# Retention and mixture of experts in one kernel: the loads of q, k and v from batch 1 on divided into 17 transfers a batch instead of 6

## The chip, the cores and the metric

The kernel runs on one core of one Trainium2 chip. The metric is the device time of one execution in microseconds (us); less is better. Engines are named as the profile names them: PE (matrix multiply) with PEld (its weight loads), DVE (VectorE), ACT (ScalarE), POOL (GpSimd) and SP (SyncE, which here only issues DMA transfers).

## The reference

A retention layer (8 batches, 8 heads, 576 positions, head size 64) feeds a mixture of experts with one expert per token (4608 tokens of 512 values, 8 experts, hidden size 1024). All data are float32.

```python
# retention, for each batch and head
scores = q @ k.T / sqrt(64)
gamma  = 1 - 2**(-5 - head)
D[i, j] = gamma**(i - j) if i >= j else 0
x = (scores * D) @ v                    # -> tokens of 8 * 64 = 512 values
# mixture of experts
xn, en = x / (|x| + 1e-6), emb / (|emb| + 1e-6)
logits = xn @ en.T / tau
e      = argmax(logits)                 # one expert a token
gate   = max(softmax(logits))
out    = gate * (relu(x @ w1[e]) @ w2[e])
```

## The kernel before, in words

The program has two stages. The retention stage is a loop over eight batches b. The expert stage follows it; it gathers the tokens of each expert and multiplies them with that expert's weights. Within each engine the order of the instructions is the order in which the Python code emits them (`manual_schedule`), SP's queue included; the semaphores between the engines are placed by the framework.

Work of one batch b in the retention stage, with the names that occur in the profile:

- `load_batch(b)` issues the batch's loads on SP: `load_qk` (L475) brings q and k, transposed, of one pair of heads p into a tile `qkt` (8 buffers, so two batches of four pairs); `load_v` (L488) brings v into `vt` (2 buffers), whose last 256 columns are the tail of positions 512 to 575; `load_k` (L483) brings k by chunks of 128 positions into `kt` (2 buffers). The order is pairs 0 and 1, v, k, pairs 2 and 3. `load_batch(1)` stands ahead of the loop, and `load_batch(b + 2)` at the end of batch b, since its buffers are those that batch b has just read.
- Batch 0 is different: its loads are cut finer and spread over SP and ACT, and its k by chunks is made on the chip (L608, L610), not loaded.
- `scale_k(b)` (L600) multiplies `kt` by a factor per position on POOL, one instruction for each of four chunks of 512 columns. It is emitted near the end of batch b - 1. `scale_q` (L619) does the same for the q of a pair, on POOL, too.
- `emit_A` (L630 on PE, L639 on DVE) makes the decayed scores of a pair; `emit_U` (L657) the products of k and v by chunk, four groups of 16 matmuls, of which each reads one chunk of the scaled `kt` and of `vt`; `emit_O` (L713) and `emit_S` (L729) the output of two pairs; `emit_At` and `emit_Ot` (L751, L768) that of the tail.
- The tokens of batch b are turned during batch b + 1 (`route_tile`, L794 on PE), copied by ACT into one of five buffers `y` in rotation (L798) and stored by SP to the scratch tensor `xd` in device memory (L800). SP also issues a quarter of an expert's first weights (L459) in batches 2 to 5.

SP works through its list in order: when a transfer has to wait (for its buffer, or for a semaphore), everything behind it waits as well. The transfers of SP's and ACT's queues use eight semaphores in rotation (DMAHW0 to DMAHW7 below), so a transfer is issued only when the one eight places earlier has landed.

```python
def load_batch(b):
    load_qk(b, 0); load_qk(b, 1)
    load_v(b); load_k(b)
    load_qk(b, 2); load_qk(b, 3)
```

Of the kernel before, what the change touches and what calls it, by code (L numbers as in the profile page):

```python
# [19 lines left out]
B, H, S, D = 8, 8, 576, 64  # L20
NP = H // 2
# [3 lines left out]
DM = H * D  # L25
# [59 lines left out]
def retention_moe(ctx: ExitStack, tc: tile.TileContext, qk, kv, w1, w2, head, cst, out):  # L85
    nc = tc.nc
# [12 lines left out]
    def cc(name):  # L99
        o, w = _C[name]  # L100
        return cs[:, o : o + w] if o < _FIRST else late["cd"][:, o - _FIRST : o - _FIRST + w]
# [346 lines left out]
    with ExitStack() as att:  # L448
# [20 lines left out]
        def load_qk(b, p):  # L469
            t = qkp.tile([P, 2, S], F32, name="qkt")  # L470
            if b == 0:
                for i, on in enumerate(both):
                    on.dma_start(out=t[:, i], in_=qk[b, p, :, i])
            else:
                nc.sync.dma_start(out=t, in_=qk[b, p])  # L475
            qkt[b, p] = t

        kt, vt_ = {}, {}
        KW = NCH * DM

        def load_k(b):
            t = a1.tile([P, KW], F32, name="kt", bufs=2)
            nc.sync.dma_start(out=t, in_=kv[b, :, :KW])  # L483
            kt[b] = t

        def load_v(b):
            t = a2.tile([P, KW + NP * D], F32, name="vt")
            nc.sync.dma_start(out=t, in_=kv[b, :, KW:])  # L488
            vt_[b] = t

        cd = late["cd"] = ap.tile([P, _CST.shape[1]], F32, name="cd")
# [12 lines left out]
        o = _C["g1"][0] - _FIRST  # L504
        nc.sync.dma_start(out=cs, in_=head)
        load_qk(0, 0)
        load_decay(0, 2 * P, nc.scalar)
        load_qk(0, 1)
        load_decay(o, _CST.shape[1] - o)
        load_decay(2 * P, 2 * P, nc.scalar)  # L510
        for i, on in enumerate(both):
            c = slice(2 * i, 2 * i + 2)
            on.dma_start(out=v0[:, c, : DM // 2], in_=v1[:, c, : DM // 2])
        load_qk(0, 2)
        load_decay(4 * P, 2 * P)
        load_decay(6 * P, 2 * P, nc.scalar)
# [361 lines left out]
        def load_batch(b):  # L878
            load_qk(b, 0)
            load_qk(b, 1)  # L880
            load_v(b)
            load_k(b)
            load_qk(b, 2)
            load_qk(b, 3)
# [57 lines left out]
        b = B - 1  # L942
# [19 lines left out]
    with ExitStack() as moe:  # L962
# [272 lines left out]
        b = B - 1  # L1235
# [53 lines left out]
    with tc.If(ntile > 0):  # L1289
        with ExitStack() as ov:  # L1290
# [9 lines left out]
                out=io8, in0=cc("iota")[:, :NE], scalar1=float(ES), scalar2=None, op0=ALU.mult  # L1300
# [4 lines left out]
                out=sel, in0=eidx_all.unsqueeze(2).broadcast_to([P, NT, NE]), in1=io8, op=ALU.is_equal  # L1305
            )
            nc.vector.tensor_tensor(
                out=sel, in0=sel, in1=ovs[:, :NE].unsqueeze(1).broadcast_to([P, NT, NE]), op=ALU.mult
# [12 lines left out]
                out=tok, in0=entry[:, :, 0], scalar1=float(P), scalar2=cc("part"), op0=ALU.mult, op1=ALU.add  # L1321
            )
            nc.vector.tensor_scalar(out=tok, in0=tok, scalar1=float(1 - P), scalar2=None, op0=ALU.add)
            for t in range(NT):
                nc.gpsimd.indirect_dma_start(
                    out=od[:, :],
                    out_offset=bass.IndirectOffsetOnAxis(ap=dsti[:, t : t + 1], axis=0),
                    in_=tok[:, t : t + 1],
# [8 lines left out]
                out=te,  # L1337
# [10 lines left out]
            with tc.For_i(0, ntile, 1) as i:  # L1348
# [9 lines left out]
                    out=of[:, 0:1], in0=ent[:, 0:1], scalar1=-1.0, scalar2=0.0, op0=ALU.add, op1=ALU.max  # L1358
                )
                nc.vector.tensor_scalar(  # L1360
                    out=of[:, 2:3], in0=ent[:, 0:1], scalar1=0.0, scalar2=BIG, op0=ALU.is_equal, op1=ALU.mult
# [6 lines left out]
                    out=go,  # L1368
                    out_offset=None,
                    in_=gd[:, :],  # L1370
# [4 lines left out]
                    out=xo,  # L1375
                    out_offset=None,
                    in_=xd[:, :],
# [8 lines left out]
                for f4 in range(NF // 4):  # L1386
                    ph = psm.tile([P, 512], F32, name="m")
                    for fi in range(4):
                        f = 4 * f4 + fi
                        for d in range(NP):  # L1390
                            o = BLK[f // NPR][d // 2] * 256 + d % 2 * P
# [11 lines left out]
                for f in range(NF):  # L1403
# [4 lines left out]
                    out=out[:, :],  # L1408
                    out_offset=bass.IndirectOffsetOnAxis(ap=oi[:, 1:2], axis=0),
                    in_=yo,  # L1410
# [61 lines left out]
```

## Time and profile before

| what | value |
|---|---|
| runs | 583.46, 584.24, 584.25 us (median 584.24) |
| profiled execution, time | 583.77 us |
| its span in the trace | 581.9 us (1.87 us lie around it) |
| retention stage | about 0 to 150 us of the span |
| PE busy | 568.6 us, 98% of the span |
| granted PE clock | full (0.999) |
| batch loads on SP from batch 1 on | 28 of `qkt` (576 KB), 7 of `vt` (1152 KB), 7 of `kt` (1024 KB) |

The share of PE is an average over two very different stages. In the retention stage both PE and the 16 DMA engines are nearly full; in the expert stage the DMA engines are busy a little over half of the time. In the tables of stretches the column "DMA share" is the mean busy share of the 16 DMA engines by their packets, and the last column what they moved. A row of the chain of waits names what the last instruction of the program waited for, step by step backwards.

### The profile page before, as it was taken

Reading aid. Unit: us, or ns where it says so; the run is one execution under the profiler, and the core shown is the slowest. Engines: PE = TensorE matmul, PEld = TensorE weight load, DVE = VectorE, ACT = ScalarE, POOL = GpSimd, SP = SyncE. Lnnn points to the kernel's source line nnn. Section 1 sums busy time; section 2 is a strip of 40 time slices with the busy share of each in tenths; the row PEclk is TensorE's granted clock in tenths of the full one; section 3 lists DMA queues with packets and bytes.
Section 4 is the critical chain, followed back from the end, with each engine's and each line's share of the span. In section 5 each row is a group of like instructions: output and inputs, shape, how many; then the busy total and the mean of one; then the engine's idle time right before and its main releaser. Section 6 shows DMA issues by size and latency. Waiting matters only on the chain.

```text
span 581.9 us, 13055 instructions
## 1 busy us (share of the span) xinstructions
PE 568.6 (98%) x5096; PEld 508.0 (87%) x5096; DVE 413.9 (71%) x829; ACT 383.6 (66%) x718; POOL 306.3 (53%) x303
## 2 busy tenths in 40 slices
PE   8999999999999999999999999999999999999995
PEld 7788888788899899889988988998899899889985
DVE  3566776667685768787877878787878778786800
ACT  1344656554748887788788778878877887876511
POOL 4474444654455668567457636645773665345021
PEclk9999999999999999999999999999999999999999
DMA  8999999972568367457544845655394366422211
GB/s 299 396 357 374 361 376 331 388 285 79 184 192 202 113 183 169 129 162 171 169 126 138 179 133 157 167 166 143 127 190 138 113 186 172 120 98 99 75 41 44
DMA packets 72689, 109.58 MB, mean 188 GB/s; under 512 B 42378, under 2 KB 44462, under 8 KB 70832
## 3 DMA queue, kind: packets, MB, share of 16 engines
q1 hardware_dynamic: 63248, 86.53, 47.7%
q0 software_dynamic: 7680, 19.95, 10.8%
q10 hardware_dynamic: 1696, 2.23, 1.2%
q8 instruction: 41, 0.67, 0.5%
q14 instruction: 24, 0.20, 0.1%
HBM read 80.62 MB, written 19.94 MB: 173 GB/s over the span
## 4 chain that ended last, share of the span: by engine, by line
PE 78%; issue 7%; DMA 5%; DVE 5%; ACT 3%; POOL 1%; SPq 0%; POOLq 0%; ACTq 0%; DVEq 0%
PE m L1154 33%; PE a L1103 14%; PE m L1103 10%; PE a L630 5%; PE m L713 4%; PE a L413 3%; PE m L794 3%; PE m L657 2%; DMA kt<-kv 2%; PE m L729 2%; PE m L821 1%; DMA cd<-cst 1%; ACT w2s L1003 1%; DMA qkt<-qk 1%; DVE hs L1069 1%
## 5 line engine op out<-in xcount | busy, mean ns | idle before, releaser
L1154 PE MATMUL m<-w2s,hs 128*128 128x512 f32 (+1 forms) x984 | 221.0, 385 | 0.4 <-DVE hs L1069 0.4
L1154 PEld LDWEIGHTS m<-w2s,hs 128*128 128x128 f32 x984 | 180.7, 188 | 38.3 <-DVE hs L1069 2.5
L1164 POOL DMA_INDIRECT out<-y,sid x40 | 43.0, 1075 | 88.7 <-ACT y L1163 63.2
L1028 POOL TENSOR_TENSOR wsum<-raw 128x256 f32<-128x256 f32 x56 | 44.1, 811 | 56.4 <-DVE hs L1069 22.3
L619 POOL TENSOR_TENSOR qkt<-qkt,gsb 128x448 f32<-128x448 f32 x32 | 36.9, 1170 | 55.1 <-PE a L630 45.4
L330 POOL DMA_INDIRECT gt<-gd,gid x40 | 50.9, 1274 | 17.1 <-issue 10.2
L1103 PE MATMUL a<-xsb,w0s 128*128 128x320 f32 x324 | 54.8, 309 | 0.0
L319 POOL DMA_INDIRECT raw<-xd,gid x40 | 39.4, 986 | 27.3 <-DVE xsb L403 16.8
L1115 DVE TENSOR_TENSOR y<-m,y 128x320 f32<-128x320 f32 x84 | 40.9, 487 | 17.4 <-PE m L1103 9.4
L1069 DVE SCALAR_TENSOR_TENSOR hs<-y,hs 128x320 fp32r<-128x320 f32 x84 | 47.5, 584 | 6.6 <-ACT hs L1074 5.5
L399 ACT CAST xsb<-raw 128x128 fp32r<-128x128 f32 x70 | 32.1, 459 | 30.2 <-DVE raw L382 29.2
L1074 ACT ACTIVATE hs<-y 128x320 fp32r<-128x320 f32 x84 | 38.9, 472 | 18.0 <-DVE y L1115 17.5
L1119 ACT COPY y<-a 128x320 f32<-128x320 f32 x84 | 35.7, 425 | 22.7 <-PE a L1103 12.4
L639 DVE TENSOR_TENSOR raw<-a,cd 128x512 f32<-128x512 f32 x64 | 39.9, 683 | 14.0 <-PE a L630 14.0
L1103 PEld LDWEIGHTS a<-xsb,w0s 128*128 128x128 f32 x324 | 49.4, 188 | 0.1
L1006 DVE TENSOR_TENSOR w2s<-raw,w2s 128x1024 fp32r<-128x1024 f32 x32 | 39.6, 1239 | 13.1 <-ACT w2s L1003 13.1
L364 ACT COPY raw<-raw 128x1024 uint16<-128x1024 uint16 x35 | 47.5, 1356 | 0.0
L375 DVE TENSOR_TENSOR raw<-raw 128x256 f32<-128x256 f32 x35 | 22.0, 628 | 35.5 <-ACT raw L364 35.5
L1163 ACT ACTIVATE y<-m,gt 128x512 f32<-128x512 f32 (+1 forms) x41 | 27.6, 673 | 23.7 <-PE m L1154 23.5
L403 DVE TENSOR_TENSOR xsb<-raw,xsb 128x128 fp32r<-128x128 f32 x70 | 39.3, 594 | 1.1 <-ACT xsb L399 0.6
L1003 ACT CAST w2s<-raw 128x1024 fp32r<-128x1024 f32 x32 | 33.5, 1046 | 7.8 <-DMA raw<-w 7.7
L630 PE MATMUL a<-qkt 64*128 64x128 f32 x512 | 34.7, 280 | 2.6 <-DMA qkt<-qk 1.5
(176 smaller groups left out, 1124.3 us busy)
## 6 DMA issues: line engine op xcount, KB each, us to landing
raw<-w SPq DMA_DIRECT2D x64, 512.0 KB, 3.7
qkt<-qk SPq DMA_DIRECT2D x28, 576.0 KB, 11.5
xd<-y SPq DMA_DIRECT2D x36, 256.0 KB, 11.2
vt<-kv SPq DMA_DIRECT2D x7, 1152.0 KB, 9.3
kt<-kv SPq DMA_DIRECT2D x7, 1024.0 KB, 10.7
qkt<-qk ACTq DMA_DIRECT2D x4, 288.0 KB, 4.4
qkt<-qk SPq DMA_DIRECT2D x4, 288.0 KB, 5.8
raw<-xd,gid POOLq DMA_INDIRECT x40, 4.0
```

What stands on the lines that cost most here:

```text
L319: nc.gpsimd.indirect_dma_start(out=t[:, XO : XO + DM], out_offset=None, in_=xd[:rows, :], in_offset=bass.IndirectOffsetOnAxis(ap=gid[:, a ...
L330: nc.gpsimd.indirect_dma_start(out=g[:, i : i + 1], out_offset=None, in_=gd[:, :], in_offset=bass.IndirectOffsetOnAxis(ap=gid[:, a : a + 1 ...
L364: nc.scalar.copy(far.bitcast(U16).rearrange("p (n h) -> p h n", h=2), near.rearrange("p (h n) -> p h n", h=2))
L630: nc.tensor.matmul(ps[h][:, c * P : (c + 1) * P], t[hs, 1, c * P : (c + 1) * P], t[hs, 0, c * P : (c + 1) * P], start=True, stop=True,)
L639: nc.vector.tensor_tensor(out=pm[:, h], in0=ps[h].rearrange("p (c n) -> p c n", c=NCH), in1=decay[:, 2 * p + h].unsqueeze(1).broadcast_to( ...
L1006: nc.vector.tensor_tensor(out=lo, in0=u, in1=hi.bitcast(F32), op=ALU.subtract)
L1028: nc.gpsimd.tensor_tensor(out=o, in0=x, in1=y, op=op)
L1069: nc.vector.scalar_tensor_tensor(out=lo, in0=part(src), scalar=0.0, in1=hi.bitcast(F32), op0=ALU.max, op1=ALU.subtract)
L1103: nc.tensor.matmul(ps[:, :HC], w[:, ws, ka, d * P : (d + 1) * P], xop(kx, xsp)[:, d, :], start=(n in (1, 2, 5) and d == 0 and k == 0), sto ...
L1115: nc.vector.tensor_tensor(out=out[:, :HC], in0=x[:, :HC], in1=out[:, :HC], op=ALU.add)
L1154: nc.tensor.matmul(ps[:, :step], hs[:, hsp, f, i * P : (i + 1) * P], w[:, ws, f, n : n + step], start=(j == 0 and k == 0), stop=(j == NF - ...
L1164: put = nc.gpsimd.indirect_dma_start(out=out[:, :], out_offset=bass.IndirectOffsetOnAxis(ap=sid[:, a : a + 1], axis=0), in_=y, in_offset=None,
```

## The change

From batch 1 on, each load is divided into pieces that have a semaphore of their own: a pair's `qkt` into its q half and its k half (2304 bytes a partition each, instead of 4608 in one), `kt` into its four chunks of 512 columns (2048 bytes, instead of 8192), and `vt` into four chunks and the tail (2048 bytes and 1024, instead of 9216). The same bytes go to the same places in the same order, all issued by SP.

```diff
         def load_qk(b, p):
             ...
             else:
-                nc.sync.dma_start(out=t, in_=qk[b, p])
+                for i in range(2):
+                    nc.sync.dma_start(out=t[:, i], in_=qk[b, p, :, i])
             qkt[b, p] = t

         def load_k(b):
             t = a1.tile([P, KW], F32, name="kt", bufs=2)
-            nc.sync.dma_start(out=t, in_=kv[b, :, :KW])
+            for o in range(0, KW, DM):
+                nc.sync.dma_start(out=t[:, o : o + DM], in_=kv[b, :, o : o + DM])
             kt[b] = t

         def load_v(b):
             t = a2.tile([P, KW + NP * D], F32, name="vt")
-            nc.sync.dma_start(out=t, in_=kv[b, :, KW:])
+            for o in range(0, KW + NP * D, DM):
+                n = slice(o, min(o + DM, KW + NP * D))
+                nc.sync.dma_start(out=t[:, n], in_=kv[b, :, KW:][:, n])
             vt_[b] = t
```

The lines behind these move by four in the new file (L600 becomes L604, L657 becomes L661).

What stands on SP for batch 1, from its v on. Before, in the brackets the semaphores that a row waits for:

```order
L488 DMA vt<-kv 128x2304 [waits DMAHW6_49]
L483 DMA kt<-kv 128x2048 [waits DMAHW7_49]
L475 DMA qkt<-qk 128x1152 [waits DMAHW0_49]
L475 DMA qkt<-qk 128x1152 [waits DMAHW1_49]
L475 DMA qkt<-qk 128x1152 [waits DMAHW2_49,PE_49,Pool_49]
```

And now:

```order
L492 DMA vt<-kv 128x512 [waits DMAHW0_49]
L492 DMA vt<-kv 128x512 [waits DMAHW1_49]
L492 DMA vt<-kv 128x512 [waits DMAHW2_49]
L492 DMA vt<-kv 128x512 [waits DMAHW3_49]
L492 DMA vt<-kv 128x256 [waits DMAHW4_49]
L485 DMA kt<-kv 128x512 [waits DMAHW5_49]
L485 DMA kt<-kv 128x512 [waits DMAHW6_49]
L485 DMA kt<-kv 128x512 [waits DMAHW7_49]
L485 DMA kt<-kv 128x512 [waits DMAHW0_49]
```

Two transfers have become nine, and the rotation of eight semaphores, which used to reach back over more than a batch's loads, now reaches back over half of them.

On POOL, `scale_k(1)` and the two `scale_q` behind it, before:

```order
L600 TENSOR_TENSOR kt<-kt,cs 128x512 [waits DMAHW7_49,DMAHW1_49]
L600 TENSOR_TENSOR kt<-kt,cs 128x512 x3
L619 TENSOR_TENSOR qkt<-qkt,gsb 128x448 [waits DMAHW4_49,PE_49]
L619 TENSOR_TENSOR qkt<-qkt,gsb 128x448 [waits DMAHW5_49,PE_49]
L619 TENSOR_TENSOR qkt<-qkt,gsb 128x448 [waits DMAHW0_49,PE_49]
```

And now:

```order
L604 TENSOR_TENSOR kt<-kt,cs 128x512 [waits DMAHW5_49,DMAHW1_49]
L604 TENSOR_TENSOR kt<-kt,cs 128x512 [waits DMAHW6_49]
L604 TENSOR_TENSOR kt<-kt,cs 128x512 [waits DMAHW7_49]
L604 TENSOR_TENSOR kt<-kt,cs 128x512 [waits DMAHW0_49]
L623 TENSOR_TENSOR qkt<-qkt,gsb 128x448 [waits DMAHW4_49,PE_49]
```

Each of the four instructions waits for its own chunk; before, the first waited for all of `kt`.

On PE, `emit_U(1)`, before:

```order
L657 MATMUL m<-vt,kt 64x64 [waits DMAHW6_49,DMAHW7_49,Activation_49,Pool_49]
L657 MATMUL m<-vt,kt 64x64 x7
L657 MATMUL m<-vt,kt 64x64 [waits Pool_49]
L657 MATMUL m<-vt,kt 64x64 x7
L657 MATMUL m<-vt,kt 64x64 [waits Activation_49,Pool_49]
L657 MATMUL m<-vt,kt 64x64 x7
L657 MATMUL m<-vt,kt 64x64 [waits Pool_49]
```

And now:

```order
L661 MATMUL m<-vt,kt 64x64 [waits DMAHW0_49,DMAHW5_49,Activation_49,Pool_49]
L661 MATMUL m<-vt,kt 64x64 x7
L661 MATMUL m<-vt,kt 64x64 [waits DMAHW6_49,DMAHW1_49,Pool_49]
L661 MATMUL m<-vt,kt 64x64 x7
L661 MATMUL m<-vt,kt 64x64 [waits DMAHW2_49,DMAHW7_49,Activation_49,Pool_49]
L661 MATMUL m<-vt,kt 64x64 x7
L661 MATMUL m<-vt,kt 64x64 [waits DMAHW3_49,DMAHW0_49,Pool_49]
```

The order of the matmuls is unchanged; three of the four groups wait for two semaphores more. Over all batches the list of PE holds 66 more waits that stand beside another wait.

## Prediction

> **What bounds the kernel now.** I read the page first: the share of PE, then the chain of waits.
>
> ```profile
> span 581.9 us, 13055 instructions
> PE 568.6 (98%) x5096; PEld 508.0 (87%) x5096; DVE 413.9 (71%) x829; ACT 383.6 (66%) x718; POOL 306.3 (53%) x303
> PE m L1154 33%; PE a L1103 14%; PE m L1103 10%; PE a L630 5%; PE m L713 4%; PE a L413 3%; PE m L794 3%; PE m L657 2%; DMA kt<-kv 2%; PE m L729 2%; PE m L821 1%; DMA cd<-cst 1%; ACT w2s L1003 1%; DMA qkt<-qk 1%; DVE hs L1069 1%
> ```
>
> PE carries the chain. The one load on it that the change touches is `kt`, at 2%. The profiled execution took 583.77 us (581.9 of span, 1.87 around it); the median of the three runs is 584.24, so 0.47 is added when I turn a sum made in the trace into a forecast.
>
> Next the chain by time, first the start, then the retention stage (columns: start, length, what).
>
> ```profile
> 14.73 10.76 DMA kt<-kv
> ...
> 27.63 2.05 POOL kt L600 x2
> ...
> 29.72 0.69 PE m L657 x16
> ...
> 62.74 2.02 PE m L657 x64
> ...
> 79.65 2.02 PE m L657 x64
> ```
>
> One transfer, `kt` of batch 1, holds the chain from 14.73 to 25.49 us; then POOL scales it and PE multiplies. From 29.72 on the chain is PE nearly throughout. So the loads set the end only in the first 30 us. The timelines of POOL and PE there (start, length, instruction, in brackets the idle time before it and who ended it):
>
> ```profile
> 25.62 4.04 POOL L600 TENSOR_TENSOR kt<-kt,cs 128x512 f32<-128x512 f32 x4 [3.57 <-DMA kt<-kv]
> 37.71 4.04 POOL L600 TENSOR_TENSOR kt<-kt,cs 128x512 f32<-128x512 f32 x4 [1.29 <-DMA kt<-kv]
> 27.49 1.92 PE L657 MATMUL m<-vt,kt 128*64 128x64 f32 x48
> 29.72 0.69 PE L657 MATMUL m<-vt,kt 128*64 128x64 f32 x16 [0.32 <-POOL kt L600]
> ```
>
> POOL stands still for 3.57 us before `scale_k(1)`, but PE has other work until 27.49. What PE loses is seen in `emit_U(1)`: its 64 matmuls run from 27.49 to 29.72 + 0.69 = 30.41, 2.92 us, where the same 64 take 2.02 in the later batches. The loss is 0.90 us.
>
> Last the DMA engines by stretch (the last two columns are the share of the 16 engines and GB/s):
>
> ```profile
> 6.00:16.00 10.00, 9.20 (x137) 7.84 (x135) 6.64 (x13) 1.55 (x2) 6.95 (x8) 1.00 1.02 347
> 16.00:38.00 22.00, 21.39 (x418) 18.06 (x418) 10.86 (x35) 8.42 (x22) 11.52 (x11) 1.00 1.01 404
> 39.60:57.20 17.60, 17.02 (x340) 14.73 (x334) 12.17 (x32) 8.54 (x23) 10.08 (x11) 1.00 0.95 355
> 57.20:74.30 17.10, 17.10 (x348) 14.90 (x343) 12.48 (x33) 10.39 (x28) 8.53 (x9) 1.00 0.96 353
> 74.30:91.70 17.40, 17.00 (x348) 14.68 (x338) 12.84 (x33) 9.53 (x24) 9.22 (x9) 1.00 1.01 374
> 91.70:109.50 17.80, 17.26 (x339) 14.88 (x332) 11.92 (x31) 10.39 (x28) 8.57 (x9) 1.00 0.93 348
> 109.50:126.00 16.50, 15.74 (x298) 13.54 (x292) 11.29 (x30) 9.39 (x23) 7.32 (x8) 1.00 0.98 369
> ```
>
> The five later rows are a batch each. The DMA engines are as full as PE: they idle 0.88, 0.68, 0, 1.25 and 0.33 us, together 3.1 us in five batches. A dearer load has little room there.
>
> **The change part by part.**
>
> *Gain: `kt` by chunks.* The chunks are 2048 bytes by 128 partitions, 0.262 MB; at the 404 GB/s of the second row one lands every 0.65 us. If the last lands when the whole did, at 25.49, the first lands at 23.5. The extra cost below (0.75 us for a whole batch, 12 of whose 17 pieces are q, k of two pairs, v and three chunks) puts that back by at most 0.5, to 24.0, the last to 26.0. POOL takes 4.04 / 4 = 1.01 us for a chunk, more than the 0.65 between landings, so it runs through and ends near 28.1 instead of 29.66. PE needs the fourth group at 27.49 + 3 x 0.5 = 29.0. `emit_U(1)` then takes 2.02 us: gain 0.90 us. It can't be more, because PE was at work until 27.49; less, down to 0, if the pieces land late. I take 0.90, since POOL has 0.9 us to spare. What is late next is PE itself, so the gain stays in the total. In batch 2, whose `kt` POOL awaited for 1.29 us, PE lost nothing (the chain has L657 there at full pace), and I count nothing.
>
> *Do the pieces come in time?* SP must issue 17 instead of 6.
>
> ```profile
> 12.69 0.81 SPq L475 DMA_DIRECT2D qkt<-qk  x2
> 14.04 0.65 SPq L488 DMA_DIRECT2D vt<-kv  x1
> 14.73 0.94 SPq L483 DMA_DIRECT2D kt<-kv  x1
> 15.72 8.48 SPq L475 DMA_DIRECT2D qkt<-qk  x4
> ...
> L475 SPq DMA_DIRECT2D qkt<-qk x28: 328/373/997, 12.7 to 112.0; - x28
> ```
>
> At a median of 0.37 us for an issue, 17 cost 6.3 us of SP's 17.4 in a batch, and SP mostly waits. The new condition is the rotation of eight semaphores: eight pieces under way are about 2.1 MB, 5.2 us at 404 GB/s. A store of 256 KB on a quiet queue lands 2.2 us after its issue (row below), so the eight reach over the latency and the queue stays full. SP gets to the `xd` stores later, but they land behind the loads now, too. Cost nothing; the cover is those 5.2 against 2.2 us.
>
> *Cost: smaller rows on the DMA engines.* No load of 2048-byte rows is in the trace. Two narrow windows stand near it: one with rows of 8 and 9 KB alone, one with stores of 2048-byte rows.
>
> ```profile
> DMA packets 49, 0.42 MB, mean 421 GB/s; under 512 B 3, under 2 KB 3, under 8 KB 3
> DMA packets 241, 0.47 MB, mean 394 GB/s; under 512 B 29, under 2 KB 29, under 8 KB 241
> ```
>
> A batch's loads are 4.59 MB: 10.90 us at 421, 11.64 at 394, so +0.75 us a batch. Bounds: 0 (only bytes count) and +2.3 (the 347 GB/s of the first stretch, whose rows are of 1024 to 2304 bytes). I take 0.75, because the rows are of the same size. It is hidden as long as each load lands before its use: +0.75 in batches 1 to 7 is 5.3 us, less the 3.1 us of idle time, so the queue is 2.2 us later at the end and PE is 0.9 earlier. Slack at the tightest places:
>
> ```profile
> 110.87 0.46 SPq L483 DMA_DIRECT2D kt<-kv  x1
> DMA to landing us min/median/max: 10.6/10.6/10.6
> 123.85 4.05 POOL L600 TENSOR_TENSOR kt<-kt,cs 128x512 f32<-128x512 f32 x4
> 61.97 8.89 SPq L800 DMA_DIRECT2D xd<-y  x5
> DMA to landing us min/median/max: 12.3/12.3/12.3
> 75.36 0.64 ACT L798 COPY y<-m 128x512 f32<-128x512 f32 x1
> 75.32 1.99 PE a L630 x32
> ```
>
> `kt` of batch 7 lands at 121.5; POOL starts at 123.85, and its fourth chunk only at 126.9. With 3.1 us less it still holds. The `y` buffer stored at 61.97 is free at 74.3 and written again at 75.36: 1.1 us of slack. By then four batches have cost 3.0 us, less the 1.6 idle: the copy may come up to 1.2 us late, but PE is busy with L630 until 77.3 and doesn't need it before. I count 0, with 0 to 2 us for the range.
>
> *Cost: more waits on PE.* 66 more waits stand beside others. The row of those that `emit_U` has today:
>
> ```profile
> L657 PEldq EVENT_SEMAPHORE  x21: 51/51/1615, 25.5 to 133.6; - x21
> ```
>
> An extra wait is an instruction of 51 ns on PE's queue. Wholly exposed they would cost 66 x 0.051 = 3.4 us; batches 3 and 4 run at 2.02 us with three of them each, so that one costs far less than its length. I count 0, bounds 0 and 3.4.
>
> Sum: -0.90 + 0 + 0 = -0.9 us: 582.9 against the profiled 583.77, 583.4 against the median. A measurement of this kernel tells about 0.2%, 1.17 us, from no change, so this forecast ends inside it.
>
> **A rule that speaks against the change.** The Trainium skill (DMA: Bandwidth & Descriptors, section Bandwidth) says to batch transfers to 1 MiB or more for 75% of peak; its section on the anatomy of one DMA fits about 2.0 us plus the bytes at 436 GB/s for one transfer issued by GpSimd. An estimate from that fit: a 256 KB transfer gets some 100 GB/s, and a batch's loads cost 11 x 2.0 = 22 us more, in place of my 0.75. The window of 256 KB stores above moved 394 GB/s on SP's queue, so there transfers overlap, and the trace doesn't agree. As a mechanism it is the last rival below.
>
> **Rivals.**
>
> 1. *Faster by more.* PE also stands still inside batches with nothing to wait for in the profile.
>
> ```profile
> 49.96 0.49 issue
> ...
> 103.37 0.47 issue
> ...
> 109.70 0.76 issue
> ```
>
> If these 1.7 us are instruction fetches held up behind 9 KB rows, shorter rows free them: -0.9 - 1.7 = -2.6, 581.6. For it: the DMA engines are full. Against: in 74.30:91.70, the fullest batch, PE is as little idle as elsewhere.
>
> 2. *The pieces come no earlier.* If the engines serve the queued pieces side by side, all four chunks land near 25.5 or later, POOL ends where it did, and the time is 584.2.
>
> 3. *Slower: the DMA queue becomes the bound.* At the upper bound of 2.3 us a batch, batches 3 to 7 lack 5 x 2.3 - 3.1 = 8.4 us; the slack of `kt` (126.9 against 121.5, 5.4 us) goes off, and +3.0 against before is left, 587.2. It decides from 1.7 us a batch on (5 x 1.7 - 3.1 = 5.4). For it: shares of 0.93 to 1.01. Against: the 394 GB/s of 2048-byte rows.
>
> 4. *Slower: the waits on PE are exposed*, 3.4 - 0.9 = +2.5, 586.7. Against: the 2.02 us.
>
> 5. *Every transfer pays its latency by itself.* 2.2 us on a quiet queue against 0.67 (0.262 MB at 394) is 1.5 us for each of 77 more transfers: 17 us a batch, as much as PE's whole batch; about 100 us slower. The row:
>
> ```profile
> DMA to landing us min/median/max: 2.2/4.2/11.2
> ```
>
> **How the numbers follow.** Forecast 0.49, spread 582.7 to 584.0, of which about a quarter lies below 583.07 (0.2% under the median). Rival 1 0.20, rival 2 0.12, rival 3 0.11, rival 4 0.07, rival 5 0.01. Faster: 0.20 and 0.13 of the forecast, 0.33. Slower: rivals 3, 4, 5, 0.19 less the mild half of 4, 0.17. Same: 0.50. The range leaves out the far end of rival 1 and the upper parts of 3 and 4: 581.9 to 585.7.
>
> **What would show it.** Right: in the profile after, `kt` is gone from the chain of waits, POOL starts `scale_k(1)` near 24, `emit_U(1)` takes 2.0 us and everything behind it stands about 0.9 us earlier; the batches keep their 17.4 us, with DMA shares near 1.0. Wrong: waits of PE, POOL or ACT for `kt`, `qkt` or `xd` in batches 4 to 7 (rival 3), `emit_U` or `emit_A` longer than 2.02 and 1.99 us (rival 4), fewer "issue" pieces (rival 1). The prediction fails above all if the rate of 2048-byte loads is far from that of the stores, which is what I took from another direction of transfer.

## The result and the profile after

The changed kernel took 587.36 us (median of 16 runs, 585.33 to 591.71), the kernel before 584.25 (16 runs, 583.41 to 586.01) beside it. The ratio is 1.006, 95% interval 1.0043 to 1.0077: 0.6% slower, where 0.1% faster was forecast, and outside the range of 581.9 to 585.7. A second timing, below, gave 1.0058 (1.0032 to 1.0084). The profiled execution took 587.0 us. The granted clock of an execution, averaged over its span, lay between 0.991 and 0.999, and those under 0.997 took 1 to 4 us longer (of the changed kernel's 16, the six under it have a median of 589.30 us, the other ten 586.66), so that "at full clock" below means the executions at 0.997 or more.

The page of the changed kernel: its span, PE's busy time, the engines' shares of the chain, and the group of the expert stage's second matrix product (last column: idle time of PE just before these instructions, and what ended most of it).

```profile
span 585.1 us, 13175 instructions
PE 568.7 (97%) x5096; PEld 508.0 (87%) x5096; DVE 414.7 (71%) x829; ACT 384.2 (66%) x718; POOL 306.6 (52%) x303
PE 72%; DVE 10%; issue 8%; ACT 4%; DMA 3%; POOL 1%; POOLq 0%; SPq 0%; ACTq 0%; DVEq 0%
L1158 PE MATMUL m<-w2s,hs 128*128 128x512 f32 (+1 forms) x984 | 221.2, 385 | 3.7 <-DVE hs L1073 3.4
```

The same group on the page of the kernel before:

```profile
L1154 PE MATMUL m<-w2s,hs 128*128 128x512 f32 (+1 forms) x984 | 221.0, 385 | 0.4 <-DVE hs L1069 0.4
```

PE's work is unchanged, 568.7 against 568.6 us. The span is 3.2 us longer, and the product of the expert stage, whose code the change doesn't touch, waits 3.3 us longer. The stretches say the same (second column: length, third: PE busy; the last two: share of the DMA engines, GB/s): five retention batches, then most of the expert stage. Before:

```profile
39.60:126.00 86.40, 84.12 (x1626) 72.73 (x1620) 60.70 (x155) 48.23 (x122) 43.72 (x42) 1.00 0.97 360
160.00:560.00 400.00, 399.38 (x2239) 361.86 (x2238) 310.43 (x542) 302.11 (x514) 222.84 (x226) 1.00 0.53 147
```

After:

```profile
39.60:126.00 86.40, 83.46 (x1652) 72.03 (x1649) 61.86 (x157) 47.25 (x118) 43.67 (x41) 1.00 1.02 372
160.00:560.00 400.00, 396.00 (x2222) 358.85 (x2221) 309.66 (x542) 301.81 (x512) 223.16 (x226) 1.00 0.53 145
```

In the 400 us of the expert stage PE lost 399.38 - 396.00 = 3.38 us; in the batches 0.66. Setting each of PE's weight loads of the one trace against the same one of the other gives the course: at 31 us the changed kernel is 1.65 us ahead, at 147 us 0.37, at 231 us 0.25; then it loses 1.82 us in one step at 289 us and 1.74 in another at 498, and 3.25 us stand at the end.

The chain of waits of the changed kernel at the places of the prediction, and at the two steps (start, length, what):

```profile
25.72 1.02 PE m L798 x8
26.75 2.01 PE m L661 x64
28.76 1.75 PE m L717 x32
...
47.78 1.20 issue
...
100.94 1.20 issue
...
281.66 4.39 DMA raw<-w
...
335.83 3.48 DMA raw<-w
...
492.23 4.43 DMA raw<-w
```

`kt` is gone from it, and `emit_U(1)` runs at full pace, as forecast. New are two loads of 4.4 us (the chain of before has one such load, of expert 3, 3.74 us long; behind it lie the 0.4 us in the row of before). Each is the load (L999 of the changed file, L995 before) of the last of an expert's four blocks of w2, here of experts 2 and 6; ACT and DVE split it (`w2hi`, `w2lo`) into the two parts that PE multiplies. The load between them, of expert 3, took 3.48.

What stands behind the first of them in the chain:

```profile
280.41 1.22 DVE w2s L1010
281.64 0.03 DVE y L1119
281.66 4.39 DMA raw<-w
286.05 0.02 issue
286.08 1.06 ACT w2s L1007
...
288.79 1.75 DVE hs L1073 x2
290.53 0.04 issue
290.58 5.51 PE m L1158 x23
```

The DMA engines during this load, by queue (packets, MB, share of the 16 engines' time). Before, 281.9 to 285.5 us:

```profile
q1 hardware_dynamic: 272, 0.52, 44.1%
q14 instruction: 1, 0.01, 0.9%
raw<-w SPq DMA_DIRECT2D x2, 512.0 KB, 3.5
```

After, 281.6 to 286.1 us:

```profile
q1 hardware_dynamic: 285, 0.58, 48.5%
q8 instruction: 1, 0.02, 1.5%
q14 instruction: 1, 0.01, 0.5%
```

A packet of queue q8 has come in: 16 KB of instructions, which began 0.94 us behind the load's issue, and again 0.97 us behind that of expert 6 (before, the nearest began 5.9 and 3.6 us behind the issue, when these loads had landed). It takes 1.5% of 16 engines for 4.5 us, 1.08 us of one engine. q8 carries 41 such packets in a run (0.67 MB). PE has some 10,300 instructions, its matmuls, weight loads and semaphore waits, which fill 41 blocks of 256 (10,496): I read it as PE's own list that is fetched there, a block of 256 instructions at a time; where PE stands in the retention stage bears this out (below). The Trainium skill (Runtime: NRT & Kernel Launch, section Instruction fetch mechanics) says that each engine's instructions are refilled in blocks of 16 KiB, 256 instructions, by a queue of the sequencer, and calls the cost of a block's end mostly hidden. The size agrees. Hidden it is from PE in the expert stage, where PE doesn't wait for the fetch and the load beside it is what lands 0.9 us late; in the retention stage it isn't, as the part on the prediction shows.

How 0.9 us of landing become 1.8 us of PE, from the timelines of DVE and POOL. Before:

```profile
288.10 0.88 DVE L1069 SCALAR_TENSOR_TENSOR hs<-y,hs 128x320 fp32r<-128x320 f32 x2
288.77 1.77 POOL L1028 TENSOR_TENSOR wsum<-raw 128x256 f32<-128x256 f32 x2 [7.51 <-DVE hs L1069]
```

After:

```profile
288.70 1.82 DVE L1073 SCALAR_TENSOR_TENSOR hs<-y,hs 128x320 fp32r<-128x320 f32 x2
288.51 1.66 POOL L1032 TENSOR_TENSOR wsum<-raw 128x256 f32<-128x256 f32 x2 [7.53 <-DVE w2s L1010]
```

The two DVE instructions `hs` that PE waits for now begin beside POOL's `wsum`, and take 1.82 us instead of 0.88. The Trainium skill (SBUF — State Buffer, section SBUF: two separate sides) says that DVE and GpSimd share a pair of ports, and that a DVE instruction with two inputs in SBUF locks out a GpSimd instruction that reads SBUF, and the reverse. The trace agrees as far as it goes: `hs<-y,hs` has two such inputs and doubles. No run here takes POOL's work away, so this half of the 1.8 us is read, not tested.

Why would the fetches move? The changed list of PE holds more instructions, because a matmul that waits for several semaphores gets further waits as instructions of their own. Of the 120 instructions that the page has more, 77 are transfers and some 45 such waits on PE; `emit_U` had 21 of them and now has

```profile
L661 PEldq EVENT_SEMAPHORE  x42: 51/51/1615, 24.7 to 132.4; - x42
```

By the row 160:560 of before, PE works off 2239 + 2238 instructions in 400 us, 0.09 us each, so 45 more of them bring a fetch some 4 us forward (seen at the two loads: 4.9 and 2.6 us): from behind the two loads into them.

### The profile page after: what moved, and what is told of

Same layout as the page of the kernel before. It is cut to its first block, busy times and chain, and to the rows that moved or that the text cites. A ratio compares the mean times of both kernels' runs of the same rounds, so it can differ in the third digit from the quotient of the medians.

```text
span 585.1 us, 13175 instructions
## 1 busy us (share of the span) xinstructions
PE 568.7 (97%) x5096; PEld 508.0 (87%) x5096; DVE 414.7 (71%) x829; ACT 384.2 (66%) x718; POOL 306.6 (52%) x303
## 4 chain that ended last, share of the span: by engine, by line
PE 72%; DVE 10%; issue 8%; ACT 4%; DMA 3%; POOL 1%; POOLq 0%; SPq 0%; ACTq 0%; DVEq 0%
PE m L1158 32%; PE a L1107 8%; PE m L1107 7%; PE a L634 6%; PE m L717 5%; PE a L413 3%; PE m L798 3%; DVE hs L1073 3%; DMA raw<-w 3%; PE m L733 2%; PE m L661 2%; DVE y L1119 2%; ACT w2s L1007 2%; PE m L825 1%; DVE w2s L1010 1%
## 5 line engine op out<-in xcount | busy, mean ns | idle before, releaser
L623 POOL TENSOR_TENSOR qkt<-qkt,gsb 128x448 f32<-128x448 f32 x32 | 36.6, 1162 | 56.4 <-PE a L634 46.6
L1073 DVE SCALAR_TENSOR_TENSOR hs<-y,hs 128x320 fp32r<-128x320 f32 x84 | 48.8, 600 | 6.4 <-ACT hs L1078 5.3
L1010 DVE TENSOR_TENSOR w2s<-raw,w2s 128x1024 fp32r<-128x1024 f32 x32 | 39.6, 1238 | 14.9 <-ACT w2s L1007 12.2
L375 DVE TENSOR_TENSOR raw<-raw 128x256 f32<-128x256 f32 x35 | 20.3, 579 | 35.0 <-ACT raw L364 35.0
L1107 PE MATMUL m<-xsb,w0s 128*128 128x320 f32 x216 | 37.1, 309 | 0.0
```

What stands on the lines that cost most here:

```text
L1010: nc.vector.tensor_tensor(out=lo, in0=u, in1=hi.bitcast(F32), op=ALU.subtract)
L1073: nc.vector.scalar_tensor_tensor(out=lo, in0=part(src), scalar=0.0, in1=hi.bitcast(F32), op0=ALU.max, op1=ALU.subtract)
L1107: nc.tensor.matmul(ps[:, :HC], w[:, ws, ka, d * P : (d + 1) * P], xop(kx, xsp)[:, d, :], start=(n in (1, 2, 5) and d == 0 and k == 0), sto ...
```

## The experiments

The theories, as the expectations name them. F: the added waits shift PE's instruction fetches onto two w2 loads. D: the smaller transfers cost in the retention stage's DMA queue. W: the added waits are exposed on PE where they stand. C: the difference belongs to the chip of the first timing. In each experiment's times "before" is the kernel before on the same chip; every variant ran 12 times. The matmuls that are put in multiply constants, and what they write is overwritten. Behind the retention stage 11, 13 and 21 of them took 0.42, 0.47 and 0.67 us.

**The shift alone, on the kernel before.** `e1_before_shift44`: 44 more instructions on PE, no load divided.

```diff
-        keep_warm(NWARM)
+        keep_warm(32)
+        for _ in range(28):
+            nc.tensor.matmul(warm[:, :8], one, one[:, :8], start=True, stop=True)
```

> The kernel before, its loads undivided, with 22 more warm-up matmuls on PE (6 of the 38 long ones are dropped and 28 of 8 columns added), so 44 more instructions on PE's list ahead of everything else. Theory F (the change adds 45 instructions to PE's list, which moves PE's 16 KB instruction fetches in the expert stage onto the third load of the second expert weights of two experts, each landing 0.9 us later and costing PE 1.75 us): slower by 2 x 1.75 = 3.5 us, about 587.7 us, and the fetches stand about 1 us behind the issue of that load near 282 and 492 us, with landings of 4.4 us instead of 3.5. Rival D (the smaller transfers of the retention stage cost the time in the DMA queue): no change, 584.2 us. Rival W (the added waits on PE are exposed where they stand): no change, 584.2 us.

**The changed kernel with the shift taken back.** `e2_after_back44`: all the divided loads, 44 instructions of PE fewer.

```diff
-        keep_warm(NWARM)
+        wide = nc.const_aps.tensor_like(1.0, like=raws[0].bitcast(BF16)[:, :304])
+        for _ in range(NWARM - 22):
+            nc.tensor.matmul(warm[:, :304], one, wide, start=True, stop=True)
```

> The changed kernel with 22 fewer warm-up matmuls (16 of 304 columns instead of 38 of 128, the same PE time), so 44 instructions fewer on PE's list and its instruction fetches in the expert stage back where they were. Theory F: the 3.5 us of the two late weight loads go, and the gain of 0.85 us at the start of retention stays: about 583.4 us. Rivals D and W: no change against the changed kernel, about 587.4 us.

**Batch 1 alone.** `e3_batch1_only`: the loads are divided only for b = 1, here `load_k` against the changed kernel's; the other two likewise.

```diff
-            for o in range(0, KW, DM):
-                nc.sync.dma_start(out=t[:, o : o + DM], in_=kv[b, :, o : o + DM])
+            step = DM if b == 1 else KW
+            for o in range(0, KW, step):
+                nc.sync.dma_start(out=t[:, o : o + step], in_=kv[b, :, o : o + step])
```

> Only batch 1's loads are divided; batches 2 to 7 are loaded as before. PE's list grows by some 7 instructions only. Theory F: the gain at the start stays (the 64 matmuls of the products of k and v of batch 1 run in 2.0 us instead of 2.9), the fetches move by only about 0.6 us and still miss the loads: 584.25 - 0.85 = 583.4 us. Rival D: six of the seven batches are undivided again, so also about 583.4 to 583.9 us. Rival W: 10 of 66 waits are left: about 583.9 us.

**The changed kernel, shifted further.** `e4_after_plus22`: 22 instructions more.

```diff
-        keep_warm(NWARM)
+        keep_warm(NWARM - 5)
+        for _ in range(16):
+            nc.tensor.matmul(warm[:, :8], one, one[:, :8], start=True, stop=True)
```

> The changed kernel with 11 more short warm-up matmuls, 22 instructions more on PE's list (5 long ones dropped, 16 short ones added). Theory F: the fetches that met the two loads now come 1.3 to 2.4 us earlier, before the loads' issue, so both landings are back at 3.5 us: about 584 us, faster than the changed kernel although it does more. Rivals D and W: no change against the changed kernel, about 587.4 us.

Measured, with before at 583.43 us (35 runs): e1 584.68, ratio 1.0011 (0.9992 to 1.003); e2 582.43, 0.9993 (0.9971 to 1.0015); e3 582.89, 0.9986 (0.9968 to 1.0004); e4 582.34, 0.9984 (0.9959 to 1.0008). e2 and e4 have every divided load, with 44 instructions fewer on PE and with 22 more; in both, the loss is gone. That refutes D as the account of the loss, since they keep its cause whole, and W, whose waits they keep whole. In e4 the fetches begin 1.1 us ahead of the two loads' issue, in e2 there is none near the first, and that of the second begins 3.55 us behind it; the loads land 3.45 to 3.54 us after issue.

e1 is a miss in size. Its fetches fall where F put them, 0.7 us behind the issue, and the loads land late. The chain and the page's group of e1:

```profile
280.10 4.50 DMA raw<-w
...
490.40 4.03 DMA raw<-w
```

```profile
L1156 PE MATMUL m<-w2s,hs 128*128 128x512 f32 (+1 forms) x984 | 221.4, 385 | 3.0 <-DVE hs L1071 2.7
```

PE loses 2.3 and 1.0 us there. But F expected some 587.7 us, and the median rose by no more than 1.25. The trace shows why: e1 entered the expert stage 2.4 us ahead of before, half of it since PE stood in "issue" for 0.8 us in the retention stage instead of 2.0. Its shift, made at the program's start, had moved the fetches of the retention stage, too. So the shift had to be made behind that stage.

**The changed kernel again**, for its time beside the next three.

> The changed kernel without any edit, to have its time beside the others of this group. Theory F (PE's instruction fetches of 16 KB, moved by the added waits, lie in front of the last w2 load of experts 2 and 6): the same fetches as before, 0.9 to 1.0 us behind the issue of these two loads, landing 4.4 us after issue, two steps of 1.7 to 1.8 us on PE; about 3.1 us over the kernel before. Rivals D (the smaller transfers cost in the retention stage) and W (the added waits are exposed where they stand) expect the same +3.1, but have no reason for steps in the expert stage. Theory C (the difference belongs to the chip of the first timing, not to the kernel): within 1 us of the kernel before.

**A shift behind the retention stage.** `e6_after_late22` is the changed kernel with 22 more instructions of PE (n = 11), `e7_before_late42` the kernel before with 42 (n = 21).

```diff
     def mm1_in(f, q):
         ...
         ps = psa.tile([P, 512], F32, name="a")
+        if (f, q) == (PAIRS[0], 0):
+            for _ in range(n):
+                nc.tensor.matmul(ps[:, :8], one, one[:, :8], start=True, stop=True)
```

> The changed kernel with 11 more matmuls of 8 columns (22 instructions of PE with their weight loads) right behind the retention stage, ahead of the first matmuls of expert 0; they are additional work. The retention stage is the changed kernel's, instruction for instruction. F: from there on PE's fetches come 22 instructions earlier, about 1.8 us, so both loads land 3.5 us after issue and the two steps are gone: 3.5 us less than the changed kernel, plus 0.3 to 1 us for the matmuls themselves; 0 to 1 us over the kernel before. D and W: nothing of the retention stage has changed, so 0.3 to 1 us more than the changed kernel, 3.5 to 4 us over the kernel before.

> The kernel before with 21 more matmuls of 8 columns (42 instructions of PE) right behind the retention stage; no load is divided. F: the fetches of the expert stage come to lie as in the changed kernel, some 0.7 to 1.1 us behind the issue of the last w2 load of experts 2 and 6, which land 4 to 4.5 us after issue; two steps of 1 to 1.8 us: 2.5 to 3.5 us, plus 0.6 to 2 us for the matmuls, 3 to 5 us over the kernel before. D and W: only the matmuls, 0.6 to 2 us over the kernel before, and no steps.

**The load issued earlier.** `e8_after_earlier`: the block whose buffer the last w2 load takes over is split one step earlier.

```diff
-                18: [(w2hi, e, 1)],
-                19: [(w2lo, e, 1)],
+                17: [(w2hi, e, 1)],
+                18: [(w2lo, e, 1)],
```

> The changed kernel with ACT's and DVE's split of w2 block 1 one step of the product order earlier (steps 17 and 18 instead of 18 and 19), in all experts. The load of the last w2 block takes over that buffer, so it is issued about 0.9 us earlier, and its use stays where it is. PE's instructions and so its fetches are those of the changed kernel. F: in experts 2 and 6 the fetch still falls into the load (now 1.8 us behind its issue, the load takes 3.5), the landing may still be 4.4 us, but 0.9 us of cover takes it up: the steps shrink from 1.8 to under 0.3 us each, 0 to 1 us over the kernel before. D and W: no change, 3.1 us over the kernel before.

Measured, with before at 584.97 us (35 runs): e5 588.76, ratio 1.0058 (1.0032 to 1.0084); e6 586.41, 1.0016 (0.9989 to 1.0043); e7 588.87, 1.0059 (1.0031 to 1.0087); e8 585.89, 1.0017 (0.9987 to 1.0048). They came 3.8, 1.4, 3.9 and 0.9 us over before, as F said but for e6, 0.4 us above what it allowed. C falls by e5. e7 divides no load and loses as much as the change; e6 divides them all, and its ratio isn't told from 1. At full clock the contrast is sharper: e5 587.88 us (4 executions), e7 587.72 (6) and e6 584.05 (5), with before at 584.44 (21).

The page's group of e5, then of e6, of e7:

```profile
L1158 PE MATMUL m<-w2s,hs 128*128 128x512 f32 (+1 forms) x984 | 221.5, 385 | 3.6 <-DVE hs L1073 3.4
```

```profile
L1163 PE MATMUL m<-w2s,hs 128*128 128x512 f32 (+1 forms) x984 | 221.3, 385 | 0.2
```

```profile
L1159 PE MATMUL m<-w2s,hs 128*128 128x512 f32 (+1 forms) x984 | 221.2, 385 | 2.2 <-DVE hs L1074 2.0
```

In e5, whose profiled execution was a long one of 591.1 us, the two loads cost PE 1.1 and 1.7 us of waits; the other 0.7 us of the row is a wait in expert 1. Of e7 the two loads in the chain, where PE's waits are 1.0 us each:

```profile
281.10 4.08 DMA raw<-w
...
490.78 4.06 DMA raw<-w
```

The profiled execution of e7 is the shortest of its twelve (584.89 us), 1.1 us over that of before: 2.0 us of steps and 0.7 of added matmuls, less what it was ahead. The rest of e7's 3.9 us is seen in no trace.

In e8 the steps are gone, but for another reason than expected: the load was issued eight matmuls earlier (some 1.2 us), and the fetch began six matmuls later, 3.0 us behind the issue, so that it hardly met the load (landing after 3.5). Whether cover takes up a fetch that does meet the load was left for the next group.

**Fetch and cover together.** `e9_earlier_late26` is e8 with n = 13, which brings the fetches back onto the load.

> The changed kernel with the split of w2 block 1 one step earlier, as in the run before, and 13 more matmuls of 8 columns (26 instructions of PE) behind the retention stage, which bring PE's fetches 2.1 us forward: in the run before they began 3.0 us behind the issue of the last w2 load of experts 2 and 6 and met it at its end, now they should begin 0.8 to 1.1 us behind it, as in the changed kernel. F with its last link (the fetch costs only what the load's cover doesn't take up): the two loads land 4.0 to 4.5 us after issue again, but they were issued 2.1 us earlier on PE's clock, so the steps stay under 0.3 us: 0 to 1.5 us over the kernel before. F without that link (any fetch in front of the load costs PE its 1 to 1.8 us, by way of something other than the landing): two steps, 3 to 4.5 us over the kernel before.

**Batch 1 alone, and the load earlier.** `e10_batch1_earlier` joins the edits of e3 and e8.

> Only batch 1's loads divided, and the split of w2 block 1 one step earlier in all experts. F: emit_U(1) at full pace as in the kernel with batch 1 alone, no steps in experts 2 and 6 wherever the fetches lie: 0.5 to 1.5 us under the kernel before; not told apart from batch 1 alone, in which no fetch met those loads. If the earlier split costs something of its own (ACT or DVE late for the products), it shows as 0.5 us or more over batch 1 alone.

Measured, with before at 586.10 us (23 runs): e9 585.44, ratio 1.0 (0.9974 to 1.0026); e10 587.84, 1.0026 (0.9995 to 1.0057). In e9 the fetches began 0.38 us behind and 0.05 ahead of the issue, a little earlier than intended, and the loads landed 4.00 and 4.04 us after issue. PE's group on its page, and what ACT waited for that load in expert 2:

```profile
L1163 PE MATMUL m<-w2s,hs 128*128 128x512 f32 (+1 forms) x984 | 219.7, 384 | 0.0
```

```profile
ACT w2s L1012 <- DMA raw<-w: 0.5, 1, 0.5
```

The landings are late and PE doesn't wait: the last link holds. e10 bears it out: two of its fetches began 0.2 us behind the last w2 loads of experts 3 and 7, these landed after 4.0 and 4.1, and PE's second product waits for nothing. (The time of e9 came out 0.7 us under before, where F allowed 0 to 1.5 over; the interval covers both.) A fetch costs PE only what the load's cover doesn't take up. In the changed kernel ACT waited 1.9 us for this load, before 1.1.

e10 is a miss: 1.7 us over before instead of 0.5 to 1.5 under, though the interval includes 1. Most of it is the clock: at full clock it is 584.97 us (5 executions) against 585.12 (13). Its trace, with a mean clock of 0.996, was 1.7 us ahead of before at 144 us and 1.3 us behind at 151. PE waits there for the routing (1.6 us, line L154 on DVE), and behind this wait the granted clock, third from the end in the row, is halved:

```profile
146.00:148.00 2.00, 2.00 (x16) 1.88 (x11) 0.06 (x1) 1.13 (x4) 0.00 (x0) 0.50 0.05 20
```

Of the twelve traces only that of e6 shows the same fall, to 0.59 and 0.56 between 146 and 150 us; in e9 a wait of the same length at the same place left the clock at 1.00. So the end of the retention stage varies in e6 to e10, and what decides it stays open. In e10's expert stage PE also stands 0.8 us at 386 us (for ACT's `y`) and 1.0 us at 490 ("issue"), both in the first product, not explained here. No version beat the kernel before by more than its interval; e3 and e4 came nearest.

All profiles in one table (landing: last w2 load of experts 2 and 6, us after its issue; wait: PE's idle time ahead of the second product, from its group; full clock: median over that of before, us, both at full clock; for the first timing the clocks of before are not on record):

| kernel | loads divided | landing | wait | ratio to before | full clock |
|---|---|---|---|---|---|
| before | no | 3.5, 3.6 | 0.4 | 1 | 0 |
| after | yes | 4.4, 4.4 | 3.7 | 1.006 | - |
| e5 (after again) | yes | 4.2, 4.9 | 3.6 | 1.0058 | +3.4 |
| e1 | no | 4.5, 4.0 | 3.0 | 1.0011 | +1.4 |
| e7 | no | 4.1, 4.1 | 2.2 | 1.0059 | +3.3 |
| e2 | yes | 3.5, 3.5 | 0.6 | 0.9993 | -0.9 |
| e4 | yes | 3.5, 3.5 | 0.2 | 0.9984 | -0.9 |
| e6 | yes | 3.6, 3.5 | 0.2 | 1.0016 | -0.4 |
| e8 | yes | 3.5, 3.5 | 0.0 | 1.0017 | +0.2 |
| e9 | yes | 4.0, 4.0 | 0.0 | 1.0 | -0.1 |
| e3 | batch 1 | 3.5, 3.5 | 0.2 | 0.9986 | -0.4 |
| e10 | batch 1 | 3.5, 3.5 | 0.0 | 1.0026 | -0.2 |

## Why the prediction was wrong, step by step

*Gain at `emit_U(1)`: right, with a smaller base.* The timelines of POOL and PE of the changed kernel:

```profile
22.97 4.05 POOL L604 TENSOR_TENSOR kt<-kt,cs 128x512 f32<-128x512 f32 x4 [1.72 <-DMA kt<-kv]
26.68 2.08 PE L661 MATMUL m<-vt,kt 128*64 128x64 f32 x64
```

POOL starts at 22.97 instead of 25.62, and PE's 64 matmuls run through. In all nine profiles with batch 1's `kt` divided POOL starts between 22.8 and 23.7, and nothing is lost. Of the three profiled kernels with the load whole, before and e1 lose 0.8 and 0.9 us, but e7 loses next to nothing: there `kt` came earlier, and POOL began at 24.66. So what the step brings lay between 0 and the loss of the profiled execution. That loss is 0.84 us, not 0.90: the prediction set 2.92 us from the timeline against 2.02 from the chain, and in the timeline the later batches take 2.08. Of the 1.65 us by which the changed kernel is ahead at 31 us, the other 0.8 arose before 8 us, in batch 0, which the change doesn't touch.

*"What is late next is PE itself, so the gain stays in the total": wrong.* Of the 1.65 us 0.3 were left at 149 us. What PE lost at 49 and 102 us came back by 110, where the kernel before stands; 1.2 us went for good between 143 and 149, at the end of the stage. PE's waits that the trace puts down to nothing, from 39 to 150 us, before, then after:

```profile
PE a L630 <- issue: 1.0, 2, 0.5
PE m L768 <- issue: 0.8, 1, 0.8
PE m L729 <- issue: 0.2, 1, 0.2
```

```profile
PE m L733 <- issue: 1.5, 2, 1.2
PE a L634 <- issue: 1.2, 1, 1.2
PE m L772 <- issue: 1.0, 1, 1.0
```

2.0 against 3.7 us, of which 1.3 lie at the end of the stage. The last, 1.0 us, is at the product (L772) at which PE waits 1.0 to 1.7 us for the routing in e6 to e10; what makes the routing late stays open.

The others are late fetches. They lie at other places of the program in every kernel, but at one place of a block: counting PE's matmuls, weight loads and semaphore waits from the start of the trace, all 31 "issue" waits of more than 0.3 us between 35 and 140 us, in the twelve profiles, end at place 193 or 194 of a block of 256. And each ends 2.2 to 2.6 us after a packet of q8 began; nowhere does PE pass the end of a block sooner than 2.2 us behind that packet. Here the wait at 49 us of the changed kernel, and q8 in the window from 46.4 to 47.8 us, whose packet began at 46.6:

```profile
48.98 0.27 PE L733 MATMUL m<-qkt,Tst 64*64 64x128 f32 x1 [1.20 <-issue]
q8 instruction: 1, 0.02, 4.8%
```

So in the retention stage PE does wait for its instructions, 1.9 us in the kernel before and 2.4 us after. Rival 1 was right in what these waits are; shorter rows didn't free them. The sums are 0.8 to 1.9 us in the three profiles with no load divided and 1.6 to 4.0 in the seven with all: the pieces may even delay the fetches, but the ranges overlap, and no run tests it.

*Cost of the smaller rows: right in that it is hidden, too dear in size.* By the rows of 39.6:126 above, the engines at full share moved 360 / 0.97 = 371 GB/s before and 372 / 1.02 = 365 now: 0.2 us for a batch of 4.59 MB, not 0.75. In the seven profiles with all loads divided this rate is 358 to 368, in the three with none 371 to 372: 0.1 to 0.5 us a batch. From 39 us on no load or store of the retention stage shows in PE's waits, and `kt` of the last batch is there when POOL wants it (no wait in brackets):

```profile
122.27 4.04 POOL L604 TENSOR_TENSOR kt<-kt,cs 128x512 f32<-128x512 f32 x4
```

So rivals 3 and 5 fell, and rival 2 by the start of POOL. The rotation of eight semaphores cost nothing, as forecast: the pieces kept the DMA engines at a share of 1.02.

*"66 more waits stand beside others ... I count 0, bounds 0 and 3.4": the step that failed.* Where they stand they do cost nothing, as I argued: `emit_U` runs in 2.01 to 2.02 us with them. I priced them by their 51 ns alone, and both ends of the range by where they stand. They are also some 45 entries in PE's list (a term that I left out), and that moved PE's 41 fetches, two of them onto loads without slack: 1.82 + 1.74 = 3.56 us. Less the 0.25 us that were left of the gain, and 0.06 of small drifts, this is the 3.25 us of the trace.

Rival 4 gives 586.7 for exposed waits, close to what was measured, and is wrong all the same: e2, e4 and e6 keep every wait and don't lose. Without the experiments its number would have looked like its proof.

## What to carry to other kernels

Whatever adds or removes instructions on an engine, a wait included, can shift everything that the engine fetches later (shown here for PE); compare the two traces instruction by instruction, and where the loss stands in code that the change doesn't touch, look at what the DMA engines carried there. A load on the path with no slack is the place to mend: issued eight matmuls earlier, some 1.2 us, it bore a fetch without cost (e9). And when an edit is worth less than 1%, try it with a few idle instructions more or fewer before you believe its sign: here 22 instructions behind the retention stage are worth 2.4 us (e6 against e5), where the change was to bring 0.9.

## What the runs showed of the hardware

- PE's instructions come in 41 packets of 16 KB through the same DMA engines as the loads. One takes about 1 us of one engine, and a 512 KB load that it falls into lands 4.0 to 4.9 us after issue instead of 3.5.
- PE reaches no block of 256 instructions sooner than 2.2 us after its packet began; where the DMA engines are full, it stood at the ends of blocks for 0.2 to 1.8 us at a time.
- In the kernels whose last w2 load has no slack, a landing late by 0.5 to 1.4 us cost PE 1.0 to 2.3 us. In each of these steps a DVE instruction behind it, which ran beside POOL's, took 1.01 us instead of 0.48.
- Behind a wait of PE of 1.6 us the granted clock fell to 0.50 and 0.56 (means of 2 us) for about 3 us in two profiles (e10, e6) and stayed at 1.00 in a third (e9).
- With loads of 1024 to 2304 bytes a partition, eight at a time on one queue, the engines at full share moved 358 to 368 GB/s, with loads of 4608 to 9216 bytes 371 to 372, the stores in the same stretch included.
